# Expert weights: held whole in SBUF and copied on chip per tile, in place of a transfer from HBM per tile

## The chip, the cores and the metric

The kernel runs on one core of a Trainium2 chip. The metric is the device time of one execution in microseconds, as a median of several runs. The profile is of a single execution, and its span is counted from the first to the last instruction; it is shorter than the timed figure, and both are given below.

## The reference

Two blocks follow one another. The first is an attention with polynomial sketches as feature map, with batch 4, 4 heads, sequence 1088 and head size 32. Its output, taken as 4352 rows of 128 numbers, goes to a mixture of 8 experts, of which each row uses one.

```python
a, b = S1 @ x, S2 @ x                      # 8 numbers each, per head and position
phi(x) = outer(a, b)                       # 64 features
kv, z = sum over s of phi(k) v, phi(k)
attn = phi(q) @ kv / (phi(q) @ z + 1e-6)   # laid out as x: (4352, 128)

logits = x @ w_gate                        # 8 experts
e = argmax(logits);  gate = softmax(logits)[e];  eom = sigmoid(x @ w_output_gate)[e]
out = gate * eom * (relu(x @ w1[e]) @ w2[e])   # w1: 128x1024, w2: 1024x128 per expert
```

All is float32. The weights of one expert are 1 MB, of all eight 8.4 MB.

## The kernel before

The rows are taken in 34 chunks of 128, mostly four chunks to a group (nine groups). For each group of k the kernel makes the sketch (`ks`), a copy of its second half (`kb`), the product (`kp`) and the sums over the sequence (`kc`); for each group of q the sketch (`qs`, `qb`, `qp`), a transposition (`qt`, `qc`), the attention itself with the logits (`qa`, `qr`, `qx`, `ql`, `qz`). Groups are joined to five routes. For each route the kernel chooses the expert of each row (`rc`), gates it (`rg`), counts positions (`rp`), works out the row's slot (`rs`, written to `sloti`) and the factor (`rf`), and sends the rows (`rd`, L524): GpSimd issues one indirect DMA per chunk, which scatters 128 rows of 144 numbers to `xs`, an array in HBM that is sorted by expert.

The experts then work on 41 tiles (`NT`) of 128 rows of one expert each. The first nine (`NE`) are early tiles: they are full of rows of routes 0 and 1 and may start before the other routes are placed. Stage `mn1`/`mt1` counts the rows and fills the first nine entries of two tables, `eti` (which expert a tile has) and `bti` (at which row of `xs` it begins); `mn4`/`mt4` fill the other 32. `mp4` (L772) scatters padding rows, and tiles from number 9 on wait for it. A tile t goes through:

- `rows(t)` (L609): SyncE loads `bti[t]` to a register (L603) and moves 128 rows from `xs` to `xin`
- `tx` (L779): TensorE transposes them, and `tv` (L784): VectorE copies the result to `xsT`
- `tu` (L791): TensorE multiplies by w1 in 8 pieces, and `th` (L798): ScalarE applies the ReLU and writes `hT`
- `td` (L805): TensorE multiplies by w2 in 8 pieces, and `ty` (L815): ScalarE scales by the row's factor
- `to` (L820): GpSimd scatters the 128 rows to the output

A float32 product of 128x128 by 128x128 shows as four matmuls in the profile's counts.

The weights lie in `wt`, three sets of buffers (`NW` = 3), each with a half for w1 and one for w2. `weights(t, a)` (L616) issues a DMA of 512 KB from HBM on SyncE's queue. The expert's number comes from `eti[t]` in a register of SyncE. A transfer is skipped where the buffer already holds that expert. The first three tiles' transfers are issued in `mt1`, those of tile t + 3 right after `tu(t)` and `td(t)`, which release the buffers. The row loads of later tiles stand on the same queue behind them.

The order of all work is written out by hand: each name with a number in the string `PLAN` is one stage of one group, route or tile, and every engine executes its part of the stages in that order. After the plan a loop over the tiles does what is left, in the order `tx(t+2), tv(t+2), tu(t+1), th(t+1), td(t), ty(t), to(t)`. Loads of k, v and q are issued on SyncE ahead of the plan, by a list of free buffers (`load`): one of q waits until an earlier group's sketch has released its buffer.

Of the kernel before, what the change touches and what calls it, by code (L numbers as in the profile page):

```python
# [13 lines left out]
F32 = mybir.dt.float32  # L14
# [10 lines left out]
NW = 3  # L25
NX = 5
# [2 lines left out]

PLAN = """
    ks0 kb0 ks1 kp0 kb1 ks2 kp1 kc0 kb2 kc1 kp2 qs0 kc2 ks3 qb0 cl0 qp0 gt0 kb3 kc2 gs0 kp3 bg0 qt0 qs1 qc0 gm0 qb1
    qs2 gc0 qp1 qa0 qb2 qp2 ks4 qr0 qx0 qt1 kb4 ql0 ks5 kp4 qc1 kc3 kb5 qz0 qs3 kp5 kc4 qb3 qa1 cl1 qp3 kc4 qr1 qx1
    gt1 qt3 gs1 ql1 gm1 qz1 qc3 ks6 rc0 gc1 ks8 kb6 qa3 kb8 kp6 rg0 rp0 qr3 qt2 rs0 rf0 qs4 qc2 qx3 rd0 kc5 qb4 ql3
    qp4 kc6 qa2 cl2 qz3 gt2 qr2 kp8 qt4 gs2 qx2 gm2 qc4 qs5 ql2 qz2 gc2 ks7 rc1 qb5 qa4 kb7 qp5 rp1 rg1 kc6 qr4 rs1
    qt5 rf1 mn1 kp7 qs7 qc5 rd1 mt1 qb7 kc7 kc8 qs6 qx4 qb6 ql4 qp6 qa5 cl3 qp7 gt3 qr5 qt6 gs3 qx5 gm3 qc6 qs8 ql5
    qz4 gc3 qt7 qb8 qz5 rc2 qa6 qc7 qa7 qr6 qp8 rg2 qx6 rp2 qr7 ql6 qx7 qt8 ql7 qc8 tx0 rs2 tx1 qa8 tv0 tv1 rf2 tx2
    qr8 tu0 tv2 rd2 qx8 ql8 qz8 tx3 th0 tu1 tv3 qz7 qz6 rc3 tx4 th1 td0 tv4 rg3 rp3 tu2 ty0 rs3 rf3 rc4 td1 th2 rg4
    mn4 tu3 mt4 ty1 rd3 td2 th3 tu4 ty2 rf4 rp4 th4 tx5 rs4 tx6 td3 tv5 tv6 rd4 mp4  # L40
"""
ROUTES = ((0, 1), (2, 3), (4, 5), (6,), (7, 8))
MARK = 1
# [8 lines left out]
def kernel(  # L52
# [12 lines left out]
    nc = tc.nc  # L65
# [4 lines left out]
    E = w_d.shape[0]  # L70
    FC = (w_d.shape[2] // 2) // 128
# [9 lines left out]
    NT = (N + E * (TS - 1)) // TS  # L81
    PR = E * TS // 128

    consts = ctx.enter_context(tc.tile_pool(name="consts", bufs=1))
    work = ctx.enter_context(tc.tile_pool(name="work", bufs=2))
# [8 lines left out]
    def ps_w(name):  # L94
        return psum.tile([128, 2, 512], F32, tag="w2", bufs=2, name=name)

    def apart(group, ins, *others):

        for g in (group,) + others:
            tc.declare_no_dep(ins.ins, group=g, reason="the rows are distinct")  # L100
        tc.add_to_no_dep_group(group, ins.ins)
# [7 lines left out]
    for i, x in enumerate((S1, S2)):  # L109
        own = slice(i * r, (i + 1) * r)  # L110
        if wide:
            x, dst, n = x.bitcast(I32), bits[own].rearrange("p d w -> p (d w)"), 2 * D
        else:
            dst, n = plain[own], D
# [33 lines left out]

    plan = [re.fullmatch(r"([a-zA-Z]+)(\d+)", w).groups() for w in PLAN.split()]
    plan = [(w, int(n)) for w, n in plan]  # L150
# [14 lines left out]
    load()  # L165


    wt = [[consts.tile([128, FC, 128], F32, tag=f"wt{a}{i}", name=f"wt{a}{i}") for a in range(2)] for i in range(NW)]

    def half(a):  # L170
        return slice(a * FC * 128, (a + 1) * FC * 128)


    ident = consts.tile([128, 128], F32, tag="ident")
# [41 lines left out]
    NE = -(-((routes[MARK][-1] + 1) * 128 - E * (TS - 1)) // TS)  # L216
# [82 lines left out]
    def spin(n):  # L299
        ps = ps_w("ps_idle")  # L300
        for i in range(n):
            nc.tensor.matmul(ps[:, 0, :128], idle, idle, start=True, stop=True)  # L302
# [226 lines left out]
    eti = consts.tile([128, NT], I32, tag="eti")  # L529
# [32 lines left out]
    def early_tiles(ps):  # L562
        full = consts.tile([128, E], I32, tag="full")
        jump = consts.tile([128, E], F32, tag="jump")
        nc.vector.tensor_tensor(full, ps, ecap, op=ALU.subtract)
        nc.vector.tensor_single_scalar(full, full, TS.bit_length() - 1, op=ALU.logical_shift_right)
        nc.vector.tensor_tensor_scan(done[:, 1:], ones[:, :E], full, 0.0, op0=ALU.mult, op1=ALU.add)
        nc.vector.tensor_scalar_min(done[:, 1:], done[:, 1:], float(NE))
        nc.vector.tensor_sub(early[:, :E], done[:, 1:], done[:, :E])
        nc.vector.tensor_scalar(jump, early[:, :E], -float(TS), float(CAP), op0=ALU.mult, op1=ALU.add)  # L570
        table(0, NE, done[:, 1:], jump, None)

    def late_tiles(ps):
        num = consts.tile([128, E], F32, tag="num")
        nc.vector.tensor_sub(num, ps, ecap)
        pd = consts.tile([128, E], F32, tag="pd")
        nc.vector.tensor_add(pd, num, padcap)
        nc.vector.tensor_mul(pd, pd, padsel)
        pa = consts.tile([128, 1], F32, tag="pa")
        nc.vector.tensor_reduce(pa, pd, axis=AX, op=ALU.add)  # L580
        pai = consts.tile([128, 1], I32, tag="pai")
        nc.vector.tensor_add(pa, pa, padoff)
        have["pai"] = pa, pai
        left = consts.tile([128, E], I32, tag="left")
        nt = consts.tile([128, E], F32, tag="nt")
        ends = consts.tile([128, E], F32, tag="ends")
        jump = consts.tile([128, E], F32, tag="jump2")
        lim = consts.tile([128, 2], F32, tag="lim")
        nc.vector.tensor_single_scalar(left, num, float(TS - 1), op=ALU.add)
        nc.vector.tensor_single_scalar(left, left, TS.bit_length() - 1, op=ALU.logical_shift_right)  # L590
        nc.vector.tensor_tensor(nt, left, early[:, :E], op=ALU.subtract)
        nc.vector.tensor_tensor_scan(ends, ones[:, :E], nt, 0.0, op0=ALU.mult, op1=ALU.add)
        nc.vector.tensor_tensor(jump, early[:, 1:], left, op=ALU.subtract)
        nc.vector.tensor_scalar(jump, jump, float(TS), float(CAP), op0=ALU.mult, op1=ALU.add)
        nc.vector.tensor_scalar_mul(lim[:, :1], early[:, :1], float(TS))
        nc.vector.tensor_scalar_add(lim[:, 1:], num[:, E - 1:], float((E - 1) * CAP))
        table(NE, NT - NE, ends, jump, lim[:, :1], lim[:, 1:])


    regs, xin, xTs, hTs = {}, {}, {}, {}  # L600

    def value(tab, t, top):
        return nc.values_load(tab[0:1, t:t + 1], engines=[mybir.EngineType.SP], min_val=0, max_val=top,  # L603
                              skip_runtime_bounds_check_because="the table is made within the bounds")

    def rows(t):
        at = value(bti, t, E * CAP - TS)
        xin[t] = work.tile([TS, W], F32, tag="xin", bufs=NE + NX + 2, name="xin")
        ins = nc.sync.dma_start(xin[t], xs[bass.ds(at, TS), :])  # L609
        if t < NE:  # L610
            tc.add_to_no_dep_group("early", ins.ins)

    def weights(t, a):
        if a == 0:
            regs[t] = value(eti, t, E - 1)
        nc.sync.dma_start(wt[t % NW][a].rearrange("p c x -> p (c x)"),  # L616
                          w_d[bass.ds(regs[t], 1), :, half(a)].rearrange("e p x -> p (e x)"),
                          cond=regs[t] != regs[t - NW] if t >= NW else None)

    def first_part():  # L620
        upper()
# [134 lines left out]
    @stage  # L756
    def mt(i):
        if i == MARK:
            early_tiles(have.pop(("mn", i)))
            for t in range(NW):  # L760
                weights(t, 0)
                weights(t, 1)
            for t in range(NE):
                rows(t)
        else:
            late_tiles(have.pop(("mn", i)))

    @stage
    def mp(i):
        pa, pai = have.pop("pai")  # L770
        nc.gpsimd.tensor_copy(pai, pa)
        apart("rows", nc.gpsimd.indirect_dma_start(  # L772
            out=xs[:, :], out_offset=bass.IndirectOffsetOnAxis(ap=pai[:, :1], axis=0),
            in_=pad.rearrange("p a b -> p (a b)"), in_offset=None), "early")

    @stage
    def tx(t):
# [8 lines left out]
    @stage  # L786
    def tu(t):
        xT = have.pop(("tv", t))
        ps = have["tu", t] = ps_w("ps_h").rearrange("p a (c x) -> p (a c) x", x=TS)
        for c in range(FC):  # L790
            nc.tensor.matmul(ps[:, c], wt[t % NW][0][:, c], xT, start=True, stop=True)  # L791
        if t + NW < NT:
            weights(t + NW, 0)

    @stage
    def th(t):
# [3 lines left out]
    @stage  # L800
    def td(t):
        hT = have.pop(("th", t))
        ps = have["td", t] = psum.tile([TS, DM], F32, tag="kvz", name="ps_y")
        for c in range(FC):
            nc.tensor.matmul(ps, hT[:, c], wt[t % NW][1][:, c], start=(c == 0), stop=(c == FC - 1))  # L805
        if t + NW < NT:
            weights(t + NW, 1)
        if t + NW >= NE - 1:
            for n in range(NE if t + NW == NE - 1 else t + NX, min(t + NX + 1, NT)):
                rows(n)  # L810

    @stage
    def ty(t):
# [14 lines left out]
    with tc.manual_schedule():  # L828
        spin(WARM)
        first_part()  # L830
        for w, n in plan:
            do(w, n)


        for t in range(NT):
            for w, n in (("tx", t + 2), ("tv", t + 2), ("tu", t + 1), ("th", t + 1), ("td", t), ("ty", t), ("to", t)):
                if n < NT and (w, n) not in did:
                    do(w, n)

# [35 lines left out]
```

## Time and profile before

| | |
|---|---|
| time, median of 3 runs | 265.01 us (263.53 to 266.76) |
| span of the profiled execution | 237.8 us |
| mean granted TensorE clock | 0.963 |
| TensorE busy | 215.5 us (91%) |
| VectorE, ScalarE, GpSimd busy | 70.0, 79.9, 82.9 us |
| queue q1 (SyncE's transfers) | 43.31 MB |
| queue q0 (GpSimd's transfers) | 5.33 MB |

The span in 40 slices of 5.9 us (the busy share of each slice in tenths):

```profile
PE   7899999998399999279999999999999999999940
DVE  4648888999346710000000000000000000000000
ACT  2133253434025343113334344243342433434410
POOL 3600017773067657721322313313223132231330
PEclk9999999999869999959999999999999999999996
DMA  6767403379248889777987899999648778310000
```

VectorE works mainly in the first 85 us, which are the attention and the routes; after that it has only the copy of each tile. GpSimd's work up to 93 us is the scatter of rows to `xs`, and after it the scatter of the output. Of the DMA share, the first quarter is mainly k, v and q, and the part from 48 us on mainly weights.

### The profile page before, as it was taken

The numbers are of one execution on the slowest core, as the hardware profiler recorded it, in microseconds if no ns is written. First come the engines' busy times: TensorE is split into PE (matmuls) and PEld (weight loads), VectorE is DVE, ScalarE is ACT, GpSimd is POOL, SyncE is SP. The second block draws the span as 40 slices with busy tenths as digits, with TensorE's granted clock in tenths as the row PEclk, the third lists the DMA queues.
The fourth block names the chain that finished last, engine by engine and source line by source line (L and its number), as shares of the span: only waits on it lengthen the run. The fifth ranks groups of instructions, "written<-read, shape, count | busy, mean of one in ns | idle before, by whom it ended". The sixth has DMA issues, their size and how long they took to land.

```text
span 237.8 us, 6864 instructions
## 1 busy us (share of the span) xinstructions
PE 215.5 (91%) x2589; PEld 210.0 (88%) x2589; DVE 70.0 (29%) x223; ACT 79.9 (34%) x148; POOL 82.9 (35%) x134
## 2 busy tenths in 40 slices
PE   7899999998399999279999999999999999999940
PEld 6889999987299999279999999999999999999930
DVE  4648888999346710000000000000000000000000
ACT  2133253434025343113334344243342433434410
POOL 3600017773067657721322313313223132231330
PEclk9999999999869999959999999999999999999996
DMA  6767403379248889777987899999648778310000
GB/s 175 274 194 251 142 4 98 97 232 383 93 127 267 305 293 339 262 228 217 302 304 220 281 303 346 296 319 334 217 145 265 222 266 273 119 37 24 0 0 0
DMA packets 21760, 49.08 MB, mean 206 GB/s; under 512 B 3594, under 2 KB 9228, under 8 KB 21728
## 3 DMA queue, kind: packets, MB, share of 16 engines
q1 hardware_dynamic: 19024, 43.31, 56.4%
q0 software_dynamic: 2544, 5.33, 6.0%
q8 instruction: 20, 0.33, 0.6%
q14 instruction: 12, 0.10, 0.1%
q10 hardware_dynamic: 160, 0.01, 0.0%
HBM read 52.75 MB, written 5.78 MB: 246 GB/s over the span
## 4 chain that ended last, share of the span: by engine, by line
PE 61%; issue 14%; POOL 10%; DMA 9%; DVE 1%; POOLq 1%; SPq 0%; ACT 0%
PE ps_h L791 24%; PE ps_y L805 21%; POOL xs L524 6%; PE ps_ab L326 5%; DMA xs<-pad,pai 3%; POOL out_dram L820 3%; DMA xs<-x,sloti 2%; PE ps_nd L410 2%; PE ps_kvz L385 2%; PE ps_xs L779 2%; DMA wt<-in_w_dram 2%; PE ps_idle L302 2%; DMA xin<-xs 2%; PE ps_qT L396 1%; DVE kp L342 1%
## 5 line engine op out<-in xcount | busy, mean ns | idle before, releaser
L791 PE MATMUL ps_h<-xsT,wt 128*128 128x128 f32 x656 | 83.7, 283 | 0.0
L805 PE MATMUL ps_y<-wt,hT 128*128 128x128 f32 x656 | 80.8, 277 | 0.5 <-ACT y L815 0.5
L791 PEld LDWEIGHTS ps_h<-xsT,wt 128*128 128x128 f32 x656 | 80.3, 200 | 0.0
L805 PEld LDWEIGHTS ps_y<-wt,hT 128*128 128x128 f32 x656 | 77.4, 194 | 0.6 <-ACT y L815 0.6
L820 POOL DMA_INDIRECT out_dram<-y,xin x41 | 39.9, 973 | 97.0 <-ACT y L815 51.5
L798 ACT ACTIVATE hT<-ps_h 128x1024 f32<-128x1024 f32 x41 | 42.0, 1025 | 74.4 <-PE ps_h L791 74.4
L784 DVE COPY xsT<-ps_xs 128x128 f32<-128x128 f32 x41 | 11.8, 291 | 132.0 <-PE ps_xs L779 132.0
L524 POOL DMA_INDIRECT xs<-x,sloti x34 | 33.7, 992 | 12.3 <-issue 8.5
L815 ACT ACTIVATE y<-ps_y,xin 128x128 f32<-128x128 f32 x41 | 15.1, 369 | 30.6 <-PE ps_y L805 30.5
L779 PE MATMUL ps_xs<-ident,xin 128*128 128x128 f32 x41 | 11.8, 293 | 9.8 <-DMA xin<-xs 9.8
L779 PEld LDWEIGHTS ps_xs<-ident,xin 128*128 128x128 f32 x41 | 6.1, 150 | 10.6 <-DMA xin<-xs 10.4
L410 PE MATMUL ps_nd<-kz,qpT 128*64 128x98 f32 x272 | 13.7, 256 | 0.0
L522 POOL TENSOR_TENSOR x<-co,ey 128x8 f32<-128x8 f32 (+2 forms) x5 | 1.1, 222 | 34.1 <-DVE rc L427 24.2
L410 PEld LDWEIGHTS ps_nd<-kz,qpT 128*64 128x64 f32 x272 | 12.4, 142 | 0.5 <-issue 0.4
L402 ACT COPY qpT<-ps_qT 128x1024 f32<-128x1024 f32 (+1 forms) x9 | 8.7, 966 | 9.9 <-PE ps_qT L396 9.9
L342 DVE TENSOR_TENSOR qp<-ps_ab,b_sb 128x1024 f32<-128x1024 f32 (+1 forms) x9 | 10.4, 1161 | 3.0 <-ACT b_sb L334 2.8
L342 DVE TENSOR_TENSOR kp<-ps_ab,b_sb 128x1024 f32<-128x1024 f32 (+1 forms) x9 | 10.3, 1159 | 2.9 <-PE ps_kvz L385 1.8
L326 PE MATMUL ps_ab<-Sb,kT 128*64 128x64 f32 x272 | 9.7, 225 | 1.0 <-DVE kp L342 0.7
L385 PE MATMUL ps_kvz<-vt,kp 128*64 128x65 f32 (+1 forms) x288 | 10.5, 223 | 0.0
L334 ACT COPY b_sb<-ps_ab 128x128 f32<-128x128 f32 (+1 forms) x18 | 4.7, 261 | 16.5 <-PE ps_ab L326 16.2
L326 PEld LDWEIGHTS ps_ab<-Sb,kT 128*64 128x64 f32 x272 | 8.7, 139 | 1.7 <-DVE kp L342 0.8
L385 PEld LDWEIGHTS ps_kvz<-vt,kp 128*64 128x64 f32 (+1 forms) x288 | 9.4, 137 | 0.5 <-PE ps_ab L326 0.2
(129 smaller groups left out, 120.6 us busy)
## 6 DMA issues: line engine op xcount, KB each, us to landing
wt<-in_w_dram SPq DMA_DIRECT2D x82, 512.0 KB
xin<-xs SPq DMA_DIRECT2D x41, 72.0 KB
vt<-in_v_dram SPq DMA_DIRECT2D x8, 260.0 KB
kT<-in_k_dram SPq DMA_DIRECT2D x8, 256.0 KB
qT<-in_q_dram SPq DMA_DIRECT2D x8, 256.0 KB
out_dram<-y,xin POOLq DMA_INDIRECT x41, 4.6
xs<-x,sloti POOLq DMA_INDIRECT x34, 5.1
vt<-in_v_dram SPq DMA_DIRECT2D x1, 130.0 KB
```

Of the source, the lines that this page charges most:

```text
L326: nc.tensor.matmul(ps[64 * t:64 * (t + 1), j * H:(j + 1) * H], src[:, j * 128 + 64 * t:j * 128 + 64 * (t + 1)], Sb[i], start=i == 0 and j ...
L342: nc.vector.tensor_mul(res[:, :n], bview(av, [list(av.ap[1]), list(av.ap[2]), [0, r]]), bview(bv, [list(bv.ap[1]), [0, r], list(bv.ap[2])]))
L385: nc.tensor.matmul(acc[b][64 * h:64 * (h + 1), s], kp[p0:p0 + np_, j * H + 2 * s + h].rearrange("s i j -> s (i j)"), vt[p0:p0 + np_, j, s] ...
L410: nc.tensor.matmul(ps[64 * t:64 * (t + 1), 2 * j + s, :VG], qpT[:, 2 * j + s, 64 * t:64 * (t + 1)], kz[(c * 128 + 64 * t) // S][:, s], sta ...
L524: apart("rows", nc.gpsimd.indirect_dma_start(out=xs[:, :], out_offset=bass.IndirectOffsetOnAxis(ap=sloti[:, j:j + 1], axis=0), in_=x[:, j] ...
L779: nc.tensor.transpose(have["tx", t], xin[t][:, :DM], ident)
L784: nc.vector.tensor_copy(have["tv", t], have.pop(("tx", t)))
L791: nc.tensor.matmul(ps[:, c], wt[t % NW][0][:, c], xT, start=True, stop=True)
L798: nc.scalar.activation(have["th", t], have.pop(("tu", t)), ACTF.Relu)
L805: nc.tensor.matmul(ps, hT[:, c], wt[t % NW][1][:, c], start=(c == 0), stop=(c == FC - 1))
L815: nc.scalar.activation(have["ty", t], have.pop(("td", t)), ACTF.Copy, scale=xin[t][:, DM:DM + 1])
L820: apart("out", nc.gpsimd.indirect_dma_start(out=out, out_offset=bass.IndirectOffsetOnAxis(ap=x.bitcast(I32)[:, DM + 1:DM + 2], axis=0), in ...
```

## The change

All experts' weights are loaded once to a tile `wall` (64 KB in each partition), by eight transfers of 1 MB, stages `wl0` to `wl7`, which stand between the stages of the attention. No tile reads weights from HBM any more. In their place stage `wa(t)` copies the w1 half of tile t's expert from `wall` to a buffer `wt0` on VectorE, and `wb(t)` the w2 half to `wt1` on ScalarE. Each of them loads `eti[t]` to a register of its own engine, and the copy's source address depends on it. The buffers still rotate among three. TensorE's order isn't changed. The loads of rows, which stood behind weight transfers, become stages of their own (`xr`); those of tiles 9 to 13 are issued at the end of the plan, later ones after `td(t)` for tile t + 5.

The change is meant to take the repeated transfers of weights off the DMA engines, and to use VectorE and ScalarE, which have time left while the tiles run.

```diff
-    gt1 qt3 gs1 ql1 gm1 qz1 qc3 ks6 rc0 gc1 ks8 kb6 qa3 kb8 kp6 rg0 rp0 qr3 qt2 rs0 rf0 qs4 qc2 qx3 rd0 kc5 qb4 ql3
...
+    gt1 qt3 gs1 ql1 gm1 qz1 qc3 ks6 rc0 gc1 ks8 wl0 wl1 wl2 kb6 qa3 kb8 kp6 rg0 rp0 qr3 qt2 rs0 rf0 qs4 qc2 qx3 rd0 kc5 qb4 wl3 wl4 ql3
+    qp4 kc6 qa2 cl2 qz3 gt2 qr2 kp8 qt4 gs2 qx2 gm2 qc4 qs5 ql2 qz2 gc2 ks7 rc1 qb5 wl5 wl6 qa4 kb7 qp5 rp1 rg1 kc6 qr4 rs1
+    qt5 rf1 mn1 kp7 qs7 wl7 qc5 rd1 mt1 qb7 kc7 kc8 qs6 qx4 qb6 ql4 qp6 qa5 cl3 qp7 gt3 qr5 qt6 gs3 qx5 gm3 qc6 qs8 ql5
+    qz4 gc3 qt7 qb8 qz5 rc2 qa6 qc7 qa7 qr6 qp8 rg2 qx6 rp2 qr7 ql6 qx7 qt8 ql7 qc8 wb0 wa0 tx0 rs2 tx1 qa8 tv0 tv1 wa1 rf2 tx2
+    qr8 tu0 tv2 rd2 qx8 ql8 qz8 tx3 th0 wb1 wa2 tu1 tv3 qz7 qz6 rc3 tx4 th1 wb2 wa3 td0 tv4 rg3 rp3 tu2 wa4 ty0 wb3 rs3 rf3 rc4 td1 th2 wb4 rg4
+    mn4 tu3 wa5 mt4 ty1 rd3 td2 th3 tu4 wa6 ty2 wb5 rf4 rp4 th4 tx5 rs4 tx6 td3 tv5 tv6 rd4 mp4 xr9 xr10 xr11 xr12 xr13
...
-    wt = [[consts.tile([128, FC, 128], F32, tag=f"wt{a}{i}", name=f"wt{a}{i}") for a in range(2)] for i in range(NW)]
...
+    wall = consts.tile([128, E, 2, FC * 128], F32, tag="wall", name="wall")
+    wt = {}
...
     def weights(t, a):
+
+        eng = (mybir.EngineType.DVE, mybir.EngineType.Activation)[a]
+        e = nc.values_load(eti[0:1, t:t + 1], engines=[eng], min_val=0, max_val=E - 1,
+                           skip_runtime_bounds_check_because="the table is made within the bounds")
+        wt[t, a] = work.tile([128, FC, 128], F32, tag=f"wt{a}", bufs=NW, name=f"wt{a}")
+        src = wall[:, bass.ds(e, 1), a].rearrange("p o x -> p (o x)")
+        dst = wt[t, a].rearrange("p c x -> p (c x)")
         if a == 0:
-            regs[t] = value(eti, t, E - 1)
-        nc.sync.dma_start(wt[t % NW][a].rearrange("p c x -> p (c x)"),
-                          w_d[bass.ds(regs[t], 1), :, half(a)].rearrange("e p x -> p (e x)"),
-                          cond=regs[t] != regs[t - NW] if t >= NW else None)
+            nc.vector.tensor_copy(dst, src)
+        else:
+            nc.scalar.copy(dst, src)
...
             early_tiles(have.pop(("mn", i)))
-            for t in range(NW):
-                weights(t, 0)
-                weights(t, 1)
             for t in range(NE):
                 rows(t)
...
+    def wl(e):
+        nc.sync.dma_start(wall[:, e].rearrange("p a x -> p (a x)"), w_d[e])
...
-            nc.tensor.matmul(ps[:, c], wt[t % NW][0][:, c], xT, start=True, stop=True)
-        if t + NW < NT:
-            weights(t + NW, 0)
+            nc.tensor.matmul(ps[:, c], wt[t, 0][:, c], xT, start=True, stop=True)
...
-            nc.tensor.matmul(ps, hT[:, c], wt[t % NW][1][:, c], start=(c == 0), stop=(c == FC - 1))
-        if t + NW < NT:
-            weights(t + NW, 1)
-        if t + NW >= NE - 1:
-            for n in range(NE if t + NW == NE - 1 else t + NX, min(t + NX + 1, NT)):
-                rows(n)
+            nc.tensor.matmul(ps, hT[:, c], wt[t, 1][:, c], start=(c == 0), stop=(c == FC - 1))
...
-            for w, n in (("tx", t + 2), ("tv", t + 2), ("tu", t + 1), ("th", t + 1), ("td", t), ("ty", t), ("to", t)):
+            for w, n in (("tx", t + 2), ("tv", t + 2), ("tu", t + 1), ("wa", t + 1 + NW), ("th", t + 1),
+                         ("td", t), ("xr", t + NX), ("ty", t), ("wb", t + NW), ("to", t)):
```

More of the change, by code (lines that the diff above doesn't have):

```diff
@@ L34 @@
     qs2 gc0 qp1 qa0 qb2 qp2 ks4 qr0 qx0 qt1 kb4 ql0 ks5 kp4 qc1 kc3 kb5 qz0 qs3 kp5 kc4 qb3 qa1 cl1 qp3 kc4 qr1 qx1
-    gt1 qt3 gs1 ql1 gm1 qz1 qc3 ks6 rc0 gc1 ks8 kb6 qa3 kb8 kp6 rg0 rp0 qr3 qt2 rs0 rf0 qs4 qc2 qx3 rd0 kc5 qb4 ql3
[L36 to L40, printed above, removed]
+    gt1 qt3 gs1 ql1 gm1 qz1 qc3 ks6 rc0 gc1 ks8 wl0 wl1 wl2 kb6 qa3 kb8 kp6 rg0 rp0 qr3 qt2 rs0 rf0 qs4 qc2 qx3 rd0 kc5 qb4 wl3 wl4 ql3
[4 more added lines that the diff above has]
+    mn4 tu3 wa5 mt4 ty1 rd3 td2 th3 tu4 wa6 ty2 wb5 rf4 rp4 th4 tx5 rs4 tx6 td3 tv5 tv6 rd4 mp4 xr9 xr10 xr11 xr12 xr13
 """
@@ L165 @@
     load()
-    wt = [[consts.tile([128, FC, 128], F32, tag=f"wt{a}{i}", name=f"wt{a}{i}") for a in range(2)] for i in range(NW)]
-    def half(a):
-        return slice(a * FC * 128, (a + 1) * FC * 128)
+    wall = consts.tile([128, E, 2, FC * 128], F32, tag="wall", name="wall")
+    wt = {}
     ident = consts.tile([128, 128], F32, tag="ident")
@@ L774, in mp, with wa, wb, xr @@
             in_=pad.rearrange("p a b -> p (a b)"), in_offset=None), "early")
+    @stage
+    def wl(e):
+        nc.sync.dma_start(wall[:, e].rearrange("p a x -> p (a x)"), w_d[e])
+    @stage
+    def wa(t):
+        weights(t, 0)
+    @stage
+    def wb(t):
+        weights(t, 1)
+    @stage
+    def xr(t):
+        rows(t)
     @stage
```

## The prediction

> **What bounds the kernel now.** I read the page first. TensorE is busy for 215.5 of 237.8 us. In the 40 slices it shows three stretches: the attention stage to 59 us, nine early expert tiles, and 32 late ones; between them are two holes. Next the chain of waits, in order of time, around those holes (columns: start us, us, what):
>
> ```profile
> 55.18 5.76 DMA xs<-x,sloti
> 60.96 0.33 SPq L609
> 61.33 0.27 SPq L603
> 61.79 1.81 DMA xin<-xs
> 63.65 0.47 PE ps_xs L779
> ...
> 66.03 3.41 PE ps_h L791 x16
> ...
> 92.77 7.81 DMA xs<-pad,pai
> 100.59 1.77 DMA xin<-xs
> 102.40 0.47 PE ps_xs L779
> 102.87 3.41 PE ps_h L791 x16
> 106.29 2.47 PE ps_y L805 x16
> 108.87 1.79 PE ps_h L791 x16
> 110.66 1.79 PE ps_y L805 x16
> ```
>
> The 59 us hole lasts until the last row scatter of route 1 has landed (5.76 us) and the first rows have come back (1.81). The 96 us hole lasts until the padding rows have landed (7.81) and then the rows of tile 9. From 108.87 a tile takes 3.69 us (start to start, 108.87 to 112.55) and TensorE doesn't pause until 226.5. No weight transfer ends a TensorE wait. So the 33.6 MB of weights that the kernel moves cost nothing directly in the long stretch. (33.6 MB is queue q1's 43.31 less 6.7 for k, q, v and 3.0 for rows: 64 of 82 transfers of 512 KB, the rest skipped as repeats.) What they can cost is time in the two holes, through the shared DMA engines. A table of stretches shows it (columns: stretch, us, busy of PE, PEld, DVE, ACT, POOL with counts, clock, DMA share, GB/s):
>
> ```profile
> 35.00:40.00 5.00, 5.00 (x102) 4.53 (x100) 4.47 (x11) 1.57 (x5) 3.81 (x4) 1.00 0.34 102
> 56.00:58.00 2.00, 2.00 (x42) 1.88 (x38) 1.85 (x6) 1.24 (x6) 0.37 (x2) 1.00 1.04 397
> 96.00:98.00 2.00, 0.54 (x5) 0.35 (x4) 0.00 (x0) 0.37 (x1) 1.39 (x3) 1.00 0.97 378
> ```
>
> At 56 and at 96 us, when the two landings were awaited, the DMA engines were full, with weights. Row scatters issued at 30 to 45 us, on idle DMA engines, landed in 2.3 to 3.5 us (median 2.8); those of 45 to 58 us took 5.1 to 6.3.
>
> [...] after both holes the table of stretches gives a clock of 0.50, and the first 16 matmuls take 3.41 us and not 1.79. [...] The trace of before has no fp32 SBUF-to-SBUF copy on VectorE in the GpSimd chains[...]; its scatters keep 1.28 us each though VectorE is 90% busy.
>
> **The change part by part.**
>
> *Traffic removed:* 33.6 MB become 8 x 1.05 = 8.4 MB, all before the tiles. After that only rows and outputs use DMA.
>
> *Traffic moved (wl0 to wl7):* SyncE is in order. wl0 to wl2 stand after the last k and v load, issued at 26.4 us; wl3, wl4 behind the q load of 35.1, wl5, wl6 behind that of 41.0, wl7 behind that of 47.1. From 30 to 35 us the DMA share is 0.01, so there is room. Full, the engines moved 383 GB/s (53.5 to 59.4 us). 8.4 MB and three q loads (0.8) make 24 us. The 16 scatters of routes 0 and 1: in the 35 to 40 row, 102 GB/s take a share of 0.34; taking the q load out leaves about 0.2, for one scatter every 1.28 us, so 0.26 us each and 4 us in all. The k and v loads in front end near 28.5, and each later pair is queued before the earlier one is through. 28.5 + 24 + 4 gives **57 us** for the last weight (estimate, 55 to 60). The last q load may land at 54 us in place of before 53; its matmuls start at 53.0, so up to 1.4 us of TensorE time moves into the 59 us hole, where it is free.
>
> *The 59 us hole:* the last scatter is issued at 55.18. Quiet, it lands in 2.8 (58.0); full, in 5.8 (61.0). Weights end between, so I take 58.7, **2.3 us** sooner. The first transpose then stands at 60.4 us, TensorE idles some 1 us rather than 3.3, and probably keeps its clock: another 1.6 us from the first 16 matmuls, if so.
>
> *Copies added:* per tile, one on VectorE (wa) and one on ScalarE (wb), 128 x 1024 fp32, each with a register load ahead. Prices: SyncE's register loads stand in the trace at 0.27 us (below), with some 0.1 of address operations. VectorE: the nearest row is a 128x128 copy from PSUM, 291 ns. [...] I take 0.69, and 1.05 with its load. ScalarE: 1.01 us as for qpT from PSUM[...]. I take 1.4 with the load.
>
> ```profile
> L603 SPq TENSOR_LOAD <-eti x41: 261/271/467, 47.6 to 212.9; - x41
> L798 ACT ACTIVATE hT<-ps_h 128x1024 f32<-128x1024 f32 x41 | 42.0, 1025 | 74.4 <-PE ps_h L791 74.4
> L815 ACT ACTIVATE y<-ps_y,xin 128x128 f32<-128x128 f32 x41 | 15.1, 369 | 30.6 <-PE ps_y L805 30.5
> L784 DVE COPY xsT<-ps_xs 128x128 f32<-128x128 f32 x41 | 11.8, 291 | 132.0 <-PE ps_xs L779 132.0
> ```
>
> In the steady stretch: ScalarE 1.03 + 0.37 + 1.4 = 2.8 us, VectorE 0.29 + 1.05 = 1.3, of 3.69. A wb waits for the second matmul group of its buffer's last tile, and behind it on ScalarE stands the next tile's ReLU, due 1.8 us later; 0.37 + 1.4 = 1.8, and that ReLU's result is needed one tile later still (2.6 us of slack). Each copy is made two to three tiles ahead. Steady cost: **none**.
>
> *wa0 and wb0* wait for all eight loads (the address is in a register). Behind wa0 on VectorE stand rs2, tv0, tv1. VectorE is free at 59.9, weights at 57: wa0 to 61.0, rs2 61.5, tv0 61.8; the first expert matmul can start near 63.4, before 66.03. **Hidden** unless weights land after 60.
>
> *Copies between 60 and 85 us:* here VectorE has little room; in before it works with about 2 us of pauses from 69.7 to 82.7 (choices of routes 3 and 4, then the late table). wa2 to wa6 add 5 x 1.05. Followed through in order, VectorE reaches rs4 (the slots of route 4) at about 82.6; in before that ended at 84.1, where TensorE's rp4 held it. TensorE gains 3 to 4 us here by the earlier start, but waits about 1 us for the count mn4, whose input comes late. The six scatters of route 4 so start **1.5 us** sooner, and the padding is issued at 91.3. I add 0.5 us for two or three copies[...] (bounds 0 and 3 x 0.69).
>
> *The 96 us hole:* the padding is 590 KB. On free DMA engines: 2.1 us (the shortest output landing) plus 590 KB at 383 GB/s = 1.5, so 3.7, and I take 4.0 in place of 7.8. The row load and cold clock stay. Tile 9 starts at 91.8 + 4.0 + 2.0 = 97.8 us; before 102.4. That is **4.6 us** sooner; the earlier hole's gain is contained in it. From there 32 tiles and the tail (229.5 to 237.8) stay as they are. I take off 0.4 for small waits: **-4.2 us**.
>
> The timed median is 265.01, 27 us above the profiled span. What is gained are waits, so I carry the microseconds over unscaled: 260.8.
>
> **The rivals.**
>
> *The wall takes the scatters' place (0.25):* for 28 us the scatters share full DMA engines; GpSimd could fall behind its 1.28 us beat, or the weights land at 61. Then the first hole ends as before, rf2 comes 1 us later, VectorE with five copies more reaches rs4 at 86.5, and the padding goes out at 95.2, lands at 99.2, tile 9 starts at 101.3: -1 us, or 264. Against it: the sum above ends at 57. For it: landings do double under full load.
>
> *The copying engines become the bound (0.17), the slower case:* if a load with its copy takes ScalarE 2.6 us rather than 1.4[...], a tile needs 1.03 + 0.37 + 2.6 = 4.0 us against 3.69, times 32 = +10, less the 4 gained: 271. Against it: 0.27 us per load on SyncE.
>
> *Both holes nearly close (0.13):* copies partly hidden behind waits, GpSimd undisturbed, clock kept in both: 2.3 us more for the second cold restart and 2 more for the padding: -8.5, or 256.5.
>
> **How the numbers follow.** Forecast 0.45 at 260.8. The low end 256.5 is the third rival; the high end 266.5 covers the first with its weights some 2.5 us late, and leaves out most of the second. Faster by over 1% means below 262.4: nine tenths of the forecast (0.40), the third rival (0.13) and a fifth of the first (0.05), 0.58. Within 1%: the rest of the forecast and most of the first rival, 0.23. Slower: the second rival and the first's bad end, 0.19.
>
> **What would show it.** Right: padding landing at 3.5 to 4.5 us, tile 9 near 98 us, a period of still 3.69 us, VectorE copies near 0.7 us, DMA share below 0.3 after 60 us. Wrong: TensorE waiting for VectorE or ScalarE after 108 us, the last scatter landing after 61, or GpSimd's beat above 1.28 us at 84 to 92 us.

## The result, and the profile after

The changed kernel takes **274.45 us** (median of 4 runs, 273.15 to 275.86), the kernel before beside it 265.88 (263.53 to 268.78): a ratio of **1.0354, 95% interval 1.0253 to 1.0455**. It is slower by 8.6 us. The forecast was 4.2 us faster.

The kernel before has no single time. The experiments below fell on four chips, and unchanged it takes about 238 us on two of them (medians 238.43 and 238.66) and about 264 us on the other two (264.33 and 264.14). The figures from before the change are of both kinds: the execution behind the profile of before took 239.49 us, the timed ones 265.01. The profile of after comes from the 264 us kind. So a time is read only against the kernel before on the same chip. Each ratio compares the executions within 1.5% of the fastest of their kernel, so that it can differ a little from the ratio of the medians.

First the 40 slices of the page of after, the rows for TensorE, the granted clock and the DMA engines (busy share, or clock, in tenths; a slice is 6.8 us):

```profile
PE   7899973973999819800899999999999999999960
PEclk9999996696699986965699999999999999999996
DMA  6585996466120110034311111111111000000000
```

The traffic is gone as intended: from the eleventh slice on no DMA digit is above 4, where before most were 7 to 9. Yet TensorE has thin slices in four places. Three of them (34 to 48 us, 55 to 68, and the 1 at about 98) are of a kind that the last section takes up. The two zeros at 116 to 129 us are the hole around the padding, and it is longer than before, when it made one slice of 2. Something other than the weights holds TensorE there. The chain of waits of after, in order of time, shows the padding and what follows it (start us, us, what):

```profile
118.71 3.53 DMA xs<-pad,pai
...
122.26 0.33 SPq L608
...
122.63 0.37 SPq L602
```

The padding rows now land in 3.53 us; before they took 7.81. In the chain of before, one row load followed the landing, and TensorE's transposition came 9.63 us after the padding was issued (102.40 - 92.77). Here it comes 11.6 us after: TensorE's timeline gives (start us, us, engine, line, operation, tiles, form, count, and in brackets the idle time before it with its releaser):

```profile
112.67 1.95 PE L821 MATMUL ps_y<-wt,hT 128*128 128x128 f32 x16
130.33 0.47 PE L797 MATMUL ps_xs<-ident,xin 128*128 128x128 f32 x1 [15.72 <-DMA xin<-xs]
130.60 3.62 PE L809 MATMUL ps_h<-xsT,wt 128*128 128x128 f32 x16
...
136.15 1.95 PE L809 MATMUL ps_h<-xsT,wt 128*128 128x128 f32 x16
...
139.83 1.95 PE L809 MATMUL ps_h<-xsT,wt 128*128 128x128 f32 x16
```

TensorE waits 15.72 us for rows, and they come 8 us after the padding has landed, not 2. Then a tile takes 139.83 - 136.15 = 3.68 us, as before. The costliest groups and the DMA issues of the page say why (groups: count, busy us, mean ns of one, idle before; issues: count, KB each):

```profile
L621 DVE COPY wt<-wall 128x1024 f32 x41 | 28.4, 693 | 55.3 <-PE ps_h L809 45.0
L623 ACT COPY wt<-wall 128x1024 f32 x41 | 42.8, 1045 | 6.9 <-remote 3.4
...
wall<-in_w_dram SPq DMA_DIRECT2D x8, 1024.0 KB
xin<-xs SPq DMA_DIRECT2D x45, 72.0 KB
```

The copies have the durations that were forecast. But there are **45 row loads for 41 tiles**; the page of before has

```profile
xin<-xs SPq DMA_DIRECT2D x41, 72.0 KB
```

The code explains the four: the final loop issues `xr(t + 5)` from t = 0 unless that stage is already in the set `did`. The rows of tiles 5 to 8 had been loaded by `rows(t)` inside `mt1`, not by a stage `xr`, so the set doesn't hold them and the loop loads them a second time. The work that the loop emits after that takes the second copy, the transposition of tile 7 first. That load reads `xs` and comes after `mp4` in the order of the code, so it waits until the padding has landed; in the chain of waits above, the landing is at 122.24 us and SyncE takes up the row loads at 122.26.

### The profile page after: what moved, and what is told of

It reads as the page before. It is cut to its first block, busy times and chain, and to the rows that moved or that the text cites. A ratio compares the mean times of both kernels' runs of the same rounds, so it can differ in the third digit from the quotient of the medians.

```text
span 272.6 us, 6577 instructions
## 1 busy us (share of the span) xinstructions
PE 225.3 (83%) x2589; PEld 215.8 (79%) x2589; DVE 97.9 (36%) x264; ACT 121.5 (45%) x189; POOL 84.1 (31%) x134
## 3 DMA queue, kind: packets, MB, share of 16 engines
q1 hardware_dynamic: 11536, 18.43, 20.7%
## 4 chain that ended last, share of the span: by engine, by line
issue 42%; PE 21%; POOL 14%; another core or an unknown queue 8%; DVE 6%; ACT 2%; DMA 2%; POOLq 1%; SPq 1%; ACTq 0%; DVEq 0%
POOL out_dram L831 12%; PE ps_ab L325 7%; PE ps_kvz L384 4%; PE ps_nd L409 2%; PE ps_qT L395 2%; POOL xs L523 2%; PE ps_h L809 2%; PE ps_y L821 1%; PE ps_idle L301 1%; DMA xs<-pad,pai 1%; ACT wt L623 1%; DVE qp L341 1%; POOLq L831 1%; DVE x L427 1%
## 5 line engine op out<-in xcount | busy, mean ns | idle before, releaser
L821 PE MATMUL ps_y<-wt,hT 128*128 128x128 f32 x656 | 82.1, 279 | 6.2 <-ACT y L826 6.2
L809 PEld LDWEIGHTS ps_h<-xsT,wt 128*128 128x128 f32 x656 | 79.0, 197 | 1.7 <-issue 1.7
L621 DVE COPY wt<-wall 128x1024 f32 x41 | 28.4, 693 | 55.3 <-PE ps_h L809 45.0
L623 ACT COPY wt<-wall 128x1024 f32 x41 | 42.8, 1045 | 6.9 <-remote 3.4
L523 POOL DMA_INDIRECT xs<-x,sloti x34 | 35.0, 1030 | 13.0 <-issue 8.8
L384 PE MATMUL ps_kvz<-vt,kp 128*64 128x65 f32 (+1 forms) x288 | 14.0, 230 | 6.0 <-issue 6.0
L384 PEld LDWEIGHTS ps_kvz<-vt,kp 128*64 128x64 f32 (+1 forms) x288 | 11.1, 140 | 8.3 <-issue 7.7
L409 PE MATMUL ps_nd<-kz,qpT 128*64 128x98 f32 x272 | 15.9, 268 | 2.0 <-issue 1.5
L409 PEld LDWEIGHTS ps_nd<-kz,qpT 128*64 128x64 f32 x272 | 13.9, 151 | 3.2 <-issue 2.3
L325 PE MATMUL ps_ab<-Sb,qT 128*64 128x64 f32 x272 | 11.5, 246 | 0.0
```

The source lines that it names most:

```text
L325: nc.tensor.matmul(ps[64 * t:64 * (t + 1), j * H:(j + 1) * H], src[:, j * 128 + 64 * t:j * 128 + 64 * (t + 1)], Sb[i], start=i == 0 and j ...
L384: nc.tensor.matmul(acc[b][64 * h:64 * (h + 1), s], kp[p0:p0 + np_, j * H + 2 * s + h].rearrange("s i j -> s (i j)"), vt[p0:p0 + np_, j, s] ...
L409: nc.tensor.matmul(ps[64 * t:64 * (t + 1), 2 * j + s, :VG], qpT[:, 2 * j + s, 64 * t:64 * (t + 1)], kz[(c * 128 + 64 * t) // S][:, s], sta ...
L523: apart("rows", nc.gpsimd.indirect_dma_start(out=xs[:, :], out_offset=bass.IndirectOffsetOnAxis(ap=sloti[:, j:j + 1], axis=0), in_=x[:, j] ...
L621: nc.vector.tensor_copy(dst, src)
L623: nc.scalar.copy(dst, src)
```

## The experiments

The theory (D in the expectations): this second load is what the change costs. The rivals: a cost of the wall's loads (L) or of the copies themselves (C). A question apart is where the 27 us between the timed figure and the profiled span of before come from.

**The kernel before, unchanged** (`before_again`), for that question.

> The kernel before, unchanged, to have a trace of an execution as slow as its timed median. The median of before (265.9 us) is 28 us over the span of its first profile (237.8), while the changed kernel's spans (271 to 274) agree with its timed runs. Theory A[...]: the span comes out near 262 to 266 us, and the 25 us lie between 30 and 105 us in waits that no engine's work explains (issue, unknown queue), as in the changed kernel. Rival (fixed cost outside the span): the span is again near 238 us and the timed median near 265.

Measured: 237.71 us, ratio 0.9981 (0.9956 to 1.0005), profiled span 235.2. Neither outcome that the expectation names came: the span stayed near 238 us, and this time the timed figure did too; the two agree to 2.5 us. So the 27 us are no fixed cost outside the span. They are a difference between comparisons on different chips. That the chip makes it is likely but not shown: none of the four stands in two of the comparisons below.

**The two halves of the change.** `loads_only` is before with the wall's eight loads added and no copy; `copies_only` is after with the loads taken out and `wall` filled with a constant by GpSimd.

```diff
 loads_only:   + wl0 ... wl7 in the plan, weights still from HBM
 copies_only:  + nc.gpsimd.memset(wall, 0.01)
               - nc.sync.dma_start(wall[:, e]..., w_d[e])
```

> The kernel before with the eight 1 MB loads of the wall added at the places of the change, and the wall not used; the tiles keep their transfers from HBM. Theory L (the wall's loads fill the DMA engines in the attention stage[...]): at least as slow as the changed kernel, 272 to 280 us, with TensorE stalling near 36 to 47 and 58 to 68 us. Theory C (the copies and their register loads do it): within 2 us of before, 264 to 268.

> The changed kernel without the wall's loads; GpSimd sets the wall to a constant in the first 30 us instead, so the experts' products are not the reference's. Theory L: no stall from 30 to 80 us and 4 us or more below before's fast profile plan, that is 232 to 240 us of span. Theory C: the stalls of 90 to 102 us stay and the time is 262 to 275.

Measured: loads alone 241.08 us, 1.0113 (1.0081 to 1.0145); copies alone 245.77 us, 1.0313 (1.0278 to 1.0348). The figures of the two expectations were written for a chip of the 264 us kind, so only the direction can be compared. The larger loss comes with the half that has the copies. But its chain of waits isn't one of copies (start us, us, what):

```profile
90.63 3.53 DMA xs<-pad,pai
94.17 0.34 SPq L609
...
94.56 0.37 SPq L603
...
95.12 0.33 SPq L609
95.49 0.27 SPq L603
...
95.95 0.33 SPq L609
96.33 0.27 SPq L603
```

Behind the padding SyncE issues one row load every 0.83 us (L603 reads the address, L609 issues), and TensorE resumes after the eighth, at 102.0. The plan puts `xr9` to `xr13` first; then come the second loads of tiles 5, 6 and 7.

**The change unchanged, on a 238 us chip** (`after_again`), and **the rows loaded once** (`rows_once`), which only tells the loop what `mt1` has done:

```diff
             for t in range(NE):
                 rows(t)
+                did.add(("xr", t))
```

> The changed kernel, unchanged, beside before on the same chip as the runs below. The trace of the changed kernel counts 45 row loads for 41 tiles: the loop's stage xr(t + 5) begins at tile 5, and the rows of tiles 5 to 8, already loaded in mt1, are loaded a second time, on SyncE's queue behind the loads of tiles 9 to 13, which wait for the padding. Theory D (that second load): TensorE stops after about tile 5 and waits some 16 us for the rows of tile 7, time 245 to 249 us where before takes 238. Rival S ([...]as in the first trace of the changed kernel): 260 us or more.

> The changed kernel with one line more, so that the rows of tiles 5 to 8 are loaded once. Theory D: tiles 6 to 8 run before the padding lands, TensorE's wait at 85 us for rows of tile 7 goes, tile 9 starts near 97 us, and the time is 233 to 236 us, 1 to 2% below before. Rival W (the copies or the wall's loads are what costs): 242 us or more.

Measured: after_again 245.68 us, 1.0297 (1.0252 to 1.0341); rows_once **233.77 us, 0.9772 (0.9725 to 0.9818)**. This one line is worth 11.9 us. TensorE's timeline of after_again around the hole:

```profile
82.83 1.95 PE L821 MATMUL ps_y<-wt,hT 128*128 128x128 f32 x16
101.54 0.48 PE L797 MATMUL ps_xs<-ident,xin 128*128 128x128 f32 x1 [16.76 <-DMA xin<-xs]
...
111.46 0.27 PE L797 MATMUL ps_xs<-ident,xin 128*128 128x128 f32 x1
```

that of before_again:

```profile
92.47 1.95 PE L805 MATMUL ps_y<-wt,hT 128*128 128x128 f32 x16
101.03 0.48 PE L779 MATMUL ps_xs<-ident,xin 128*128 128x128 f32 x1 [6.62 <-DMA xin<-xs]
```

and that of rows_once (the profiled execution is one of its longest, 236.6 us):

```profile
92.96 1.95 PE L822 MATMUL ps_y<-wt,hT 128*128 128x128 f32 x16
99.45 0.47 PE L798 MATMUL ps_xs<-ident,xin 128*128 128x128 f32 x1 [4.54 <-DMA xin<-xs]
```

What resumes TensorE at 101.54 is the transposition of tile 7; at 101.03 (before_again) and 99.45 (rows_once) it is that of tile 9, which in after_again stands at 111.46. With the second loads, TensorE stops at 84.8 us, and the early tiles' work, meant to fill the time until the padding is in, is left for later. Loaded once, that work runs to 94.9, and 4.54 us of waiting remain. Row loads are 41, and queue q1 moves 18.14 MB in place of 18.43: four times 72 KB less.

**Without the wall's loads too** (`rows_once_copies_only`):

> As rows_once, without the wall's loads (GpSimd sets the wall to a constant, so the experts' products are not the reference's). Theory D: 13 us below copies_only, near 233 us; the difference to rows_once is what the loads of the wall cost in the attention stage (expected 0 to 3 us).

Measured: 232.97 us, 0.9789 (0.9742 to 0.9835), equal to rows_once within its interval. In the repaired kernel the 8.4 MB cost nothing that this measures. The loss of 1.1% in loads_only appears where tiles fetch their own weights on top; there TensorE waited 5.37 us for the first rows, 2.86 in before_again.

**Place on the queue, or the wait?** `reload_ahead` is the change with `xr9` to `xr13` taken out of the plan, so that the second loads come first:

```diff
-    ... tv5 tv6 rd4 mp4 xr9 xr10 xr11 xr12 xr13
+    ... tv5 tv6 rd4 mp4
```

> The changed kernel with its 45 row loads, but with xr9 to xr13 taken from the end of the plan, so that the second loads of tiles 5 to 8 stand on the queue before the first load that waits for the padding. Theory D: the doubled load itself is cheap (72 KB each); what costs is its place behind the padding, so within 2 us of rows_once. Rival (the doubled load itself): no better than the changed kernel.

Measured: 241.21 us, 1.0124 (1.0077 to 1.0171). The expectation failed: 4.5 us came back, not 11.9. They fit five loads of 0.83 us, and TensorE's longest wait for rows is 12.6 us in place of 16.8. The waits of SyncE's queue show the rest (total us, times, longest us):

```profile
SPq L608 <- DMA xs<-pad,pai: 27.4, 1, 27.4
```

The second load waits for the padding itself, though it now stands first on the queue. Both matter: some 4.5 us for the five loads ahead of it, and the larger part because an early tile now depends on the padding at all.

**The second loads put into the kernel before** (`before_reload`), on a 264 us chip:

```diff
-    ... tv5 tv6 rd4 mp4
+    ... tv5 tv6 rd4 mp4 xr5 xr6 xr7 xr8
```

> The kernel before with one thing of the change alone: at the end of the plan the rows of tiles 5 to 8 are loaded a second time. Theory D: the second load is a reading of xs behind the padding's scatter, so it waits until the padding has landed, tiles 7 and 8 wait with it, and two tiles (7.4 us) and more move behind the hole at 94 us: 245 to 252 us. Rival (what hurts in the changed kernel is the copies, and the doubled loads only add to it): within 2 us of before.

Measured: 269.07 us, 1.0208 (1.0130 to 1.0287): slower by 4.7 us with no wall and no copy. That is clear of the rival, but less than the 7 us and more that were expected. TensorE's timeline has a gap of the same kind:

```profile
108.88 1.95 PE L809 MATMUL ps_y<-wt,hT 128*128 128x128 f32 x16
121.43 0.47 PE L783 MATMUL ps_xs<-ident,xin 128*128 128x128 f32 x1 [10.59 <-DMA xin<-xs]
```

So the second load alone costs time in either kernel. How long this wait is in the unchanged kernel on such a chip was not recorded, so the cost is read from the times.

**Better than the repaired kernel?** Two edits to rows_once: `slots_first` computes route 4's slots before two of VectorE's copies (`wa5`, `wa6`) and before the late table (`mn4`, `mt4`); `wall_later` moves two of the wall's loads behind, off the queue ahead of the last q load; a third kernel has both.

```diff
 slots_first:  - mn4 tu3 wa5 mt4 ... wb5 rf4 rp4 th4 tx5 rs4 tx6
               + rp4 tu3 rs4 rf4 mn4 wa5 mt4 ... wb5 th4 tx5 tx6
 wall_later:   - qb5 wl5 wl6 qa4 ... qs7 wl7
               + qb5 qa4 ... qs7 wl5 wl6 wl7
```

> rows_once with the slots and factors of route 4 (rp4, rs4, rf4) put ahead of the count and of the late table (mn4, mt4) in the plan. If the second hole is set by VectorE reaching rs4 late, behind the copies and the table, the six scatters of route 4 start at 80 to 81 us instead of 85, the padding lands 3 to 4 us earlier, TensorE's wait of 4.5 us before tile 9 shrinks to under 1.5 us[...]: 226 to 230 us. If GpSimd's earlier scatters or the padding's landing set it, no more than 1 us below rows_once.

> rows_once with wl5 and wl6 moved behind the last q load, beside wl7. In rows_once the last q load (issued at 47.4) lands at 54.5 to 55.7 behind them, and TensorE waits 0.5 to 1.4 us for it. If this wait reaches the end, 0.5 to 1.5 us below rows_once, unless the wall itself then lands after 60 us and the first copy waits for it.

> Both moves together: the gains add if they are in different stretches, so 225 to 229 us.

On a 264 us chip: 0.9988 (0.9949 to 1.0027), 0.9981 (0.9952 to 1.0011), 0.9990 (0.9959 to 1.0021). None differs from before. rows_once was not beside them, and the expectations in us were written for a chip of the other kind, so whether the edits do what was expected can't be read from this. A second comparison had rows_once beside two of them:

> The changed kernel with the rows of tiles 5 to 8 loaded once, a second time beside other kernels of the same chip. Theory D (the second load of those rows is what the change costs): below the kernel before, ratio 0.97 to 0.98 where the kernel before takes about 238 us; where it takes about 264 us the gain may be lost among the stalls that no engine's work explains, ratio 0.99 to 1.00. Rival (the first 0.977 was a matter of that one comparison): a ratio above 1.0.

> The same, with route 4's slots computed before the seventh to ninth wall copies and weights are in VectorE's stream. If route 4's slots set the end of the second hole: the scatters, the padding and tile 9 come 1 to 1.5 us earlier, and the time is 0.4 to 0.6% below the kernel with rows loaded once in this comparison. If the early tiles' end sets it: equal within 0.3%.

> Both the earlier slots and the wall's loads 5 and 6 moved beside load 7. If the queries' last load behind the wall costs TensorE its 1.4 us at 55 us: another 0.4 to 0.6% below the kernel with earlier slots alone. If that wait is hidden by the route's later chain: equal within 0.3%.

It fell on the other 264 us chip: rows_once 0.9875 (0.9798 to 0.9953), slots_first 0.9982 (0.9953 to 1.0012), both edits 0.9958 (0.9931 to 0.9984). The six executions of rows_once spread from 259.1 to 264.4 us, and their median of 263.28 is just 0.9 us under that of before. On this chip the repaired kernel gains 0.3% by the medians and 1.25% by the ratio, with an interval of 0.5 to 2.0%. The gain expected of slots_first over rows_once did not come; whether either edit helps was not settled, and on a 238 us chip they were not tried.

## Why the prediction was wrong, point by point

**The step that failed** is "The row load and cold clock stay. Tile 9 starts at 91.8 + 4.0 + 2.0 = 97.8 us". It took for granted that only tile 9 and later depend on the padding, and that TensorE has tiles 5 to 8 to work on until then. The runs showed instead that tiles 5 to 8 depend on it too, through their second loads: in after_again TensorE stops 16.8 us and resumes at 101.5 with tile 7, and tile 9 follows only at 111.5; loading the rows once took 11.9 us off the time. The diff made row loads stages of their own; the prediction followed weights, scatters and copies through SyncE's order but not these loads, and didn't count them. Its own sum could have caught it in the profile of after: 43.31 - 33.6 + 8.4 = 18.1 MB for q1, where the page has 18.43. Its list of what would show it wrong names TensorE's waits on VectorE and ScalarE, the last scatter and GpSimd's beat, and no wait on a row load.

The balance on the 238 us chips: TensorE's waits for `xin` were 9.9 us in before_again and 17.1 in after_again, 7.2 us more. The spans of these two executions differ by 9.1 us, the medians of after_again and of before beside it by 7.0. So the longer wait is most of the loss; the rest was not worked out.

The other steps, on the same kind of chip. The forecast was made from the first profile of before, and before_again shows how far a second one lies from it:

| step | before, before_again | forecast | after_again | rows_once |
|---|---|---|---|---|
| VectorE copy, ScalarE copy | none | 0.69, 1.01 us | 0.69, 1.05 | 0.69, 1.05 |
| first expert matmul (timeline) | 65.8, 65.2 | near 63.4 | 62.4 | 65.15 |
| slots of route 4 done | 84.1, 82.0 | about 82.6 | 80.7 | 83.5 |
| padding issued | 92.8, 90.6 | 91.3, or 91.8 with the 0.5 us for copies | 90.2 | 93.0 |
| padding's landing takes | 7.81, 8.58 | 4.0 us | 3.51 | 4.47 |
| transposition of tile 9 | 102.4, 101.0 | 97.8 | 111.5 | 99.45 |
| period of a tile | 3.69, 3.68 | 3.69 | 3.68 | 3.68 |
| time against before | 0 | -4.2 us | +7.0 | -4.9 |

- **The 59 us hole** closed in after_again as forecast: the first transposition stands at 60.05 us (forecast 60.4, 62.24 in before_again), and TensorE idles 0.4 us at most. The granted clock was 1.00 from 58 to 70 us, where before_again has 0.86; in before it was 0.50 from 64 to 66. That the clock would hold over a pause of 1 us was the author's estimate; this run, with its shorter pauses, does not show it. The first 16 expert matmuls take 1.95 us in the timeline, against 3.62 in before and 2.49 in before_again. (These 16 records are one tile's product by w1 in 8 pieces, so a product of 128x128 by 128x128 shows as two, and not as four as said above; in all, before has 656 matmuls by w1 for 41 tiles.) In rows_once's profiled execution the last q load, behind the wall on the queue, held TensorE for 1.36 us, a case that the forecast had named and taken to be free. There 64 matmuls behind it (L409) took 4.34 us, 2.94 in after_again, and the granted clock from 58 to 70 us was 0.90; in that execution the first expert matmul came no sooner than in before_again.
- **The copies** take 693 ns on VectorE and 1045 ns on ScalarE in after, against 0.69 and 1.01 us in the forecast. The 1.01 us stands in the trace of before as ScalarE's copy to `qpT` (L402, 1014 ns). The 0.69 us was the author's estimate: no line of before shows a copy of this size on VectorE.
- **The copies and GpSimd.** The forecast set 0.5 us aside for a delay of GpSimd by the copies, an estimate of the author for which the trace of before has no instance. In after_again GpSimd's instructions beside such copies are longer. Some lines of VectorE's timeline, then of GpSimd's:

```profile
69.83 0.69 DVE L621 COPY wt<-wall 128x1024 f32 x1
...
79.02 0.69 DVE L621 COPY wt<-wall 128x1024 f32 x1 [0.24 <-PE ps_h L809]
81.00 0.68 DVE L621 COPY wt<-wall 128x1024 f32 x1
```

```profile
70.14 1.23 POOL L523 DMA_INDIRECT xs<-x,sloti  x1 [0.30 <-issue]
71.67 0.98 POOL L523 DMA_INDIRECT xs<-x,sloti  x1 [0.30 <-DVE mx L467]
...
78.57 1.26 POOL L523 DMA_INDIRECT xs<-x,sloti  x1 [0.31 <-issue]
80.14 0.98 POOL L523 DMA_INDIRECT xs<-x,sloti  x1 [0.30 <-issue]
81.13 0.60 POOL L520 COPY x<-ids 128x6 int32<-128x6 int32 x1
```

Scatters beside a copy from `wall` take up to 1.32 us; in before_again, which has no such copies, the scatters of the same routes take 0.97 to 1.03. The small copy at 81.13 takes 0.60 us, its like in before_again 0.21. On the way to the padding this adds 0.4 us, and 0.1 more in one scatter of route 4 (1.08 us): the size that was set aside.

- **The slower rival** gave 271 us, near the result, for a reason that did not happen. After 108 us TensorE waited for ScalarE once, for 0.5 us, in after_again.
- **The first rival** (the wall in the scatters' place) finds no support in the times: taking the wall's loads out of rows_once moved the median by 0.8 us, within its interval.
- **The 27 us between the timed median and the span** were carried over as if they were part of every execution. In before_again the timed figure and the span are 2.5 us apart. Nor does the forecast's gain carry over: in the one comparison of rows_once where before takes 264 us, the medians differ by 0.9 us.

So the forecast's sum holds for the kernel with rows loaded once (-4.9 us between the medians, -4.2 forecast), on a chip of the kind that the profile of before came from; the kernel that was changed had a fault beside it that cost 11.9 us. Its parts are shown only in part. The profiled execution of rows_once took 236.6 us, no less than that of before_again (236.98 us): the padding went out later than there (93.0 against 90.6), only its landing was faster (4.47 us against 8.58), and tile 9 came 1.6 us sooner. A shorter execution of rows_once was not profiled. That of rows_once_copies_only, which has no loads of the wall, took 232.16 us and has tile 9 at 95.7.

## What to carry to other kernels

When a diff turns a side effect into a stage of its own, count its instances and find what each waits for before pricing anything: four loads of 72 KB that nobody needed cost 11.9 us, more than the 4.9 us that were gained with 25 MB of traffic saved. In these kernels a load that is issued again after a later write to the same array takes on that write's wait (27.4 us in reload_ahead), even where the data it needs have long been there. After the run, compare the counts of DMA issues (45 against 41) first: here that one number led to the cause.

## What was not expected of the hardware

The same program took 238 or 264 us, each chip seen in one comparison. Between the executions after and after_again the whole difference lies ahead of the hole around the padding: TensorE stops for it at 84.8 us in after_again and at 114.6 in after, and from the transposition of tile 7 to the end of the span both take some 142.5 us (142.8 and 142.3). The thin slices of after fall together with GpSimd's row scatters (35 to 45, 56 to 66 and 84 to 101 us). Much of the idle time there has no engine's work behind it: TensorE's idle time is put to "issue" (6.0 us in 12 pauses before the matmuls of `ps_kvz` in after), or at 98 us to ScalarE (5.7 us), which waited for a queue that the profile doesn't name. TensorE's timeline of before_reload on a 264 us chip:

```profile
59.86 0.35 PE L385 MATMUL ps_kvz<-vt,kp 128*64 128x65 f32 x4 [0.41 <-issue]
60.63 0.34 PE L385 MATMUL ps_kvz<-vt,kp 128*64 128x65 f32 x3 [0.43 <-issue]
61.35 0.36 PE L385 MATMUL ps_kvz<-vt,kp 128*64 128x65 f32 x4 [0.38 <-issue]
62.10 0.35 PE L385 MATMUL ps_kvz<-vt,kp 128*64 128x65 f32 x4 [0.40 <-issue]
```

and GpSimd's at the same time:

```profile
57.84 1.03 POOL L524 DMA_INDIRECT xs<-x,sloti  x1 [0.59 <-POOL x L522]
59.17 0.99 POOL L524 DMA_INDIRECT xs<-x,sloti  x1 [0.30 <-issue]
60.46 0.98 POOL L524 DMA_INDIRECT xs<-x,sloti  x1 [0.30 <-issue]
```

TensorE gets about four matmuls every 0.74 us and waits for nothing that is recorded, while GpSimd keeps its beat of 1.28 us with row scatters. In the profile of before the same line runs without a gap (48 matmuls in a row in 1.57 us from 46.90). What TensorE waits for there, and why only in some comparisons, no run here shows. It stays open.

A register load takes much the same on each engine: 0.304 us on VectorE and 0.278 on ScalarE (medians of 41 each in after_again), 0.271 on SyncE before.
